# Twelve small stores of an attention and MoE kernel: from SyncE's queue to GpSimd's

## The chip, the cores and the metric

The kernel runs on one core of one Trainium2 chip. The metric is the device time of one execution in microseconds (us). A core has five instruction queues that run side by side and wait for each other by semaphores: TensorE (PE, with its weight loads PEld), VectorE (DVE), ScalarE (ACT), GpSimd (POOL) and SyncE (SP). SP does no arithmetic here; it issues DMA transfers. ACT and POOL can issue them too, from the same in-order queue in which their arithmetic stands.

## The reference, cut to what matters

```python
scores = scale * np.matmul(q, k.transpose(0, 1, 3, 2))      # 4 batches, 8 heads, 576 x 576, head size 64
cum = np.cumsum(np.maximum(s, 0.0), axis=-1)                # one running sum per head
bias = -(cum[:, :, :, None] - cum[:, :, None, :])
scores = np.where(causal, -1e9, scores + np.minimum(bias, 0.0))
attn = softmax(scores)                                      # with 1e-9 in the denominator
x = (attn @ v) put together as 2304 x 512
h = max(x @ w1, x @ w2, x @ w3) @ w_out                     # 512 -> 768 -> 512
y = ((h @ w_a) * (h @ w_b)) @ w2_out                        # 512 -> 1536 -> 512
```

All of it is float32. The running sums `cum` enter the scores as extra rows of the contraction: a row of sums on the side of k against a row of ones on the side of q, and the other way round.

## The kernel before, in words

**Stages.** Attention runs over four batches, each cut in two steps: R = 0 is the first 256 queries, R = 1 the other 320, and each step takes four pairs of heads. So there are eight steps. While a step's attention runs, TensorE is filled up with the first MoE layer's matmuls (line 826, tile `g`) of an earlier step. From about the middle of the run the second half follows: w_out, then the second MoE layer, with its products formed in a Strassen-like scheme.

**Plain and split scores.** In the first three steps (`NPLAIN = 3`) the scores are plain float32 matmuls, whose extra rows come from the DRAM tiles `ck` and `cq` (lines 500 to 520). From the fourth step on they are split: every operand is a rounded high part and a rest, and the sums are split as well. The high and low sums lie in DRAM tiles `kt` and `qt`, and rows of the tiles `KB2` and `QA2` are loaded from them by `k_tails` (line 572) and `q_tails` (line 577), on ACT's queue for the steps R = 1 and for the first pair of a step, on SP's else.

**The stores.** `store_tails` (line 209) makes the high part `hi` by an ACT cast (line 212) of the sums `cum`, leaves the rest in `cum` by a DVE subtraction (line 213), and calls `store_sums` (line 200) twice: six DMAs from `hi` and six from `cum`, to `kt` and `qt`. Each DMA reads 16 partitions. `store_sums` is called a third time earlier, in the lead-in (line 1207), for `ck` and `cq`. `hi` lies in the space that `KB2` takes later, `cum` in that of `KB1`; `preset` (line 224) fills `QA1`, `KB2` and `QA2` with constants by eight POOL memsets (lines 230 to 239).

**What else stands in the two queues.** SP issues nearly all loads: the weights of the first MoE layer, `wraw` (line 255, three staging buffers `wst`, each freed once the high and low part of a weight block have been made by lines 266, 269, 270, 81 and 92), and the q, k and v of coming pairs (line 509). POOL multiplies each block of exponentials by the reciprocal of its row sum (line 642, tiles `F` and `FJ`). The product is transposed by TensorE (lines 778, 780, 791) and goes from there into the product with v (line 760, `fpv`).

**The order.** The kernel lists its work as entries with a position in steps (`stream`), sorted, with priorities (`tc.high_priority`): attention of the first two steps 300, weights 200, MoE matmuls, `store_tails` and `preset` 0. A planner then fixes each queue's order at build time by its own estimate of durations; `issue_after` puts instructions behind a given one. On the chip each queue runs strictly in that order. `store_tails` has position 1.3 and `preset` 1.6; both are put behind the end of the last softmax listed before them:

```python
stream.append((1.3, 0, lambda: behind_sm(store_tails)))
stream.append((1.6, 0, lambda: behind_sm(preset)))
```

Of the kernel before, what the change touches and what calls it, by code (L numbers as in the profile page):

```python
# [29 lines left out]
def kernel(  # L30
# [18 lines left out]
    nc = tc.nc  # L49
# [18 lines left out]
    Q0 = 256  # L68
# [6 lines left out]
    def f(ap):  # L75
        return ap.bitcast(F32)
# [62 lines left out]
    kt = dram.tile([2, SR, 2, S], F32, name="kt")  # L139
    qt = dram.tile([2, SR, 2, N1], F32, name="qt")  # L140
# [26 lines left out]
    def early(nm, dt=F32):  # L167
        w = 2 * S if nm in ("KB1", "KB2") else QW
        return ap_.tile([P, w], dt, tag=nm, bufs=1, name=f"e{nm}")

    cum, sraw = early("KB1"), early("KB2")
# [25 lines left out]
            op0=ALU.mult, op1=ALU.add,  # L197
        )

    def store_sums(dk, dq, t):  # L200
        nc.sync.dma_start(dk[:, :, :Q0], t[64:80, : 2 * Q0].rearrange("r (h c) -> r h c", h=2))
        a, b = t[64:80, tl_], t[80:96, tl_]
        nc.sync.dma_start(dk[:, 0, Q0:], a)
        nc.sync.dma_start(dk[:, 1, Q0:], b)
        nc.sync.dma_start(dq[:, 0], a)
        nc.sync.dma_start(dq[:, 1, 0:64], b[:, 256:])
        nc.sync.dma_start(dq[:, 1, 64:], b[:, :256])

    def store_tails():
        hi = early("KB2", F32R)  # L210
        c = slice(0, 2 * Q0 + N1)
        nc.scalar.copy(hi[rr, c], cum[rr, c])
        nc.vector.tensor_tensor(cum[rr, c], cum[rr, c], f(hi[rr, c]), op=ALU.subtract)
        store_sums(kt[0], qt[0], f(hi))
        store_sums(kt[1], qt[1], cum)

    def heads(t, r0, r1, n):

# [797 lines left out]
    for stp in range(nsteps):  # L1016
        b, R = divmod(stp, 2)
# [18 lines left out]
    def behind_sm(fn):  # L1036
        with ExitStack() as es:
            for e_ in done_sm[-1]:
                es.enter_context(tc.issue_after(e_))
            fn()  # L1040

    stream.append((1.3, 0, lambda: behind_sm(store_tails)))
    stream.append((1.6, 0, lambda: behind_sm(preset)))

# [37 lines left out]
    def lead_in():  # L1082
# [119 lines left out]
        with tc.high_priority(4000):  # L1202
            fs(0)
            fs(1)
            with tc.issue_after(pend[-1][-1]):
                scan_tails()
            lead_rows.append(lambda: store_sums(ck, cq, cum))
            fetch(NP)
            fs(2)
            ts(0)  # L1210
            fs(3)
            sm_b(pend.pop(0))
            ts(1)
            pv(0)
            ts(2)
            pv(1)
            fetch(NP + 1)
            ts(3)
            wn()
            pv(2)  # L1220
            wn()
            sp(1)
            pv(3)
            wn(NL - 2)
# [731 lines left out]
```

## Time and profile before

| what | us |
|---|---|
| median of 3 runs | 881.88 |
| lowest, highest | 881.17, 883.26 |
| profiled execution, whole | 881.39 |
| profiled execution, span from first to last instruction | 879.3 |
| TensorE busy | 869.2 |
| VectorE busy | 631.2 |
| ScalarE busy | 401.7 |
| GpSimd busy | 198.1 |

The granted clock of TensorE is 1.00 of full speed over the span. Busy time counts what an engine computes; issuing a DMA and waiting on a semaphore are not counted. A row with a "q" behind the engine (SPq, ACTq) is the queue's own instruction, such as the issue of a DMA.

### The profile page before, as it was taken

What the parts mean: (1) busy time and instruction counts of PE and PEld (TensorE: products, weight loads), DVE (VectorE), ACT (ScalarE), POOL (GpSimd) and SP (SyncE); (2) the same over time, 40 slices, a digit from 0 to 9 for tenths busy, and PEclk for the clock granted to TensorE, in tenths of its full rate; (3) what the DMA queues carried; (4) which work ended last, traced back from release to release, by engine and by line L of the source; (5) the groups of instructions that cost most, each with busy time, mean ns of one, the idle gap of its engine ahead of it and who ended that gap; (6) DMA issues with size and microseconds to landing.
All of it is one profiled execution on the core that took longest, in us unless ns stands there. A gap on an engine that the chain in (4) does not pass through costs nothing.

```text
span 879.3 us, 16771 instructions
## 1 busy us (share of the span) xinstructions
PE 869.2 (99%) x6024; PEld 827.2 (94%) x6024; DVE 631.2 (72%) x1435; ACT 401.7 (46%) x872; POOL 198.1 (23%) x317
## 2 busy tenths in 40 slices
PE   8999999999999999999999999999999999999998
PEld 6667999899999998999999999999999999999998
DVE  7886555676767666665798867676766859987873
ACT  6686745575656545563554323232323224433321
POOL 6224312333423323200002111111111310322211
PEclk9999999999999999999999999999999999999999
DMA  7675634265224853474201134444442253353331
GB/s 226 197 204 174 179 121 127 74 189 152 64 86 137 245 171 117 135 289 154 108 12 61 46 111 150 151 150 151 150 150 102 103 188 121 110 164 127 97 120 49
DMA packets 68371, 120.07 MB, mean 137 GB/s; under 512 B 7024, under 2 KB 50784, under 8 KB 68288
## 3 DMA queue, kind: packets, MB, share of 16 engines
q1 hardware_dynamic: 61096, 111.60, 40.4%
q10 hardware_dynamic: 7192, 7.40, 2.5%
q8 instruction: 48, 0.79, 0.4%
q14 instruction: 35, 0.29, 0.1%
HBM read 87.95 MB, written 31.01 MB: 135 GB/s over the span
## 4 chain that ended last, share of the span: by engine, by line
PE 92%; DMA 2%; DVE 2%; ACT 1%; issue 1%; SPq 0%; POOL 0%; POOLq 0%; ACTq 0%; DVEq 0%
PE X L1322 29%; PE g L826 24%; PE Z L1322 15%; PE Y L1322 8%; PE fpv L760 5%; PE t L778 2%; DMA wraw<-in_moe_w_dram 2%; PE s L650 2%; PE s L651 2%; PE f L694 1%; PE ft L733 1%; PE W L1322 1%; PE sj L684 1%; PE tj L791 1%; PE sj L685 1%
## 5 line engine op out<-in xcount | busy, mean ns | idle before, releaser
L826 PE MATMUL g<-Xh,hg 128*128 128x256 f32 (+1 forms) x576 | 174.2, 306 | 1.9 <-POOL hg L88 0.8
L826 PE MATMUL g<-Xl,hg 128*128 128x256 f32 (+1 forms) x576 | 173.6, 302 | 0.0
L826 PE MATMUL g<-Xh,lg 128*128 128x256 f32 (+1 forms) x576 | 172.4, 301 | 0.0
L826 PEld LDWEIGHTS g<-Xh,hg 128*128 128x128 f32 x576 | 108.3, 189 | 5.9 <-ACT hg L81 1.5
L826 PEld LDWEIGHTS g<-Xh,lg 128*128 128x128 f32 x576 | 108.5, 189 | 3.0 <-issue 1.1
L826 PEld LDWEIGHTS g<-Xl,hg 128*128 128x128 f32 x576 | 108.8, 189 | 1.8 <-issue 0.7
L88 POOL TENSOR_SCALAR wh<-wval 128x256 fp32r<-128x256 f32 x77 | 39.9, 528 | 273.9 <-DVE wval L354 224.9
L1322 PE MATMUL X<-xh,wh 128*128 128x384 f32 x288 | 97.3, 338 | 0.0
L1322 PE MATMUL X<-xl,wh 128*128 128x384 f32 x288 | 96.9, 336 | 0.0
L1322 PE MATMUL X<-xh,wl 128*128 128x384 f32 x288 | 96.8, 337 | 0.0
L1322 PE MATMUL X<-woh,slot 128*128 128x256 f32 x408 | 76.6, 281 | 0.5 <-ACT ob L1369 0.5
L642 POOL TENSOR_SCALAR P<-P,rs 128x128 f32<-128x128 f32 (+2 forms) x80 | 50.4, 634 | 96.1 <-DVE rs L638 66.6
L367 DVE TENSOR_TENSOR slot<-hraw,slot 128x768 fp32r<-128x768 f32 x60 | 60.4, 1033 | 13.8 <-POOL slot L88 11.0
L367 DVE TENSOR_TENSOR u<-Z,u 128x384 f32<-128x384 f32 x72 | 39.6, 552 | 37.0 <-ACT u L1369 27.3
L1322 PEld LDWEIGHTS X<-woh,slot 128*128 128x128 f32 x408 | 64.3, 189 | 0.7 <-ACT ob L1369 0.7
L628 ACT ACTIVATE P<-P,nm 128x128 f32<-128x128 f32 (+2 forms) x80 | 46.6, 583 | 35.4 <-DVE nm L621 25.1
L835 DVE TENSOR_TENSOR hf<-g,hf 128x256 f32<-128x256 f32 (+1 forms) x96 | 43.6, 454 | 22.7 <-PE g L826 17.2
L1322 PE MATMUL X<-wol,slot 128*128 128x256 f32 x204 | 56.9, 280 | 0.0
L81 ACT ACTIVATE slot<-hraw 128x768 fp32r<-128x768 f32 x39 | 32.5, 845 | 51.4 <-DVE hraw L367 24.4
L1322 PEld LDWEIGHTS X<-xh,wh 128*128 128x128 f32 x288 | 54.0, 188 | 0.8 <-DVE u L367 0.3
L1322 PEld LDWEIGHTS X<-xl,wh 128*128 128x128 f32 x288 | 54.1, 188 | 0.0
L1322 PEld LDWEIGHTS X<-xh,wl 128*128 128x128 f32 x288 | 54.0, 188 | 0.0
(228 smaller groups left out, 2201.1 us busy)
## 6 DMA issues: line engine op xcount, KB each, us to landing
hT<-u SPq DMA_DIRECT2D x72, 192.0 KB
hraw<-hT SPq DMA_DIRECT2D x36, 384.0 KB
wraw<-in_moe_w_dram SPq DMA_DIRECT2D x18, 512.0 KB
wraw<-in_moe_w_out_dram SPq DMA_DIRECT2D x18, 512.0 KB
kraw<-in_kT_dram SPq DMA_DIRECT2D x24, 288.0 KB
wraw<-in_moe_w_a_dram SPq DMA_DIRECT2D x12, 512.0 KB
wraw<-in_moe_w_b_dram SPq DMA_DIRECT2D x12, 512.0 KB
st<-h1T SPq DMA_DIRECT2D x24, 192.0 KB
```

The source lines that it names most:

```text
L81: return nc.scalar.activation(o, i, AF.Copy, scale=scale)
L88: nc.gpsimd.tensor_scalar(o, i, scale, 1.0, op0=ALU.mult, op1=ALU.mult)
L367: return {"V": nc.vector, "P": nc.gpsimd}[e].tensor_tensor(o, a, b, op=op)
L628: e_ = nc.scalar.activation(pt[:, c0:c1], pt[:, c0:c1], AF.Exp, bias=first, scale=-1.0, accum_out=sm[:, g : g + 1],)
L642: n_ = nc.gpsimd.tensor_scalar(pt[:, c0:c1], pt[:, c0:c1], rs[:, g : g + 1], 1.0, op0=ALU.mult, op1=ALU.mult,)
L650: nc.tensor.matmul(ps, QA1[:, qs], KB1[:, h, ksl], start=True, stop=False)
L651: nc.tensor.matmul(ps, QA2[:, qs], KB2[:, h, ksl], start=False, stop=True)
L760: e_ = nc.tensor.matmul(ps[h * D : h * D + D, c0:n], w, x, start=(t == 0), stop=(t == len(mm[h]) - 1),)
L778: nc.tensor.transpose(ps[:, j * P : j * P + P], pt[:, j * P : j * P + P], ident)
L826: nc.tensor.matmul(ps[:, :n], w[:, kk, :], x[:, kk, :], start=(i == 0), stop=(i == len(mm) - 1),)
L835: st["V"] = nc.vector.tensor_tensor(hf, ps[:, :n], hf, op=ALU.max)
L1322: e_ = nc.tensor.matmul(ps[:, :n], w, x, start=(first and i == 0), stop=(i == len(mm) - 1), skip_group_check=not first,)
```

## The change

Both calls of `store_sums` in `store_tails` pass GpSimd's queue, so that their twelve DMAs are issued by POOL. The call of the lead-in (line 1207) keeps SP. What is stored, from where and to where is the same.

```diff
-    def store_sums(dk, dq, t):
-        nc.sync.dma_start(dk[:, :, :Q0], t[64:80, : 2 * Q0].rearrange("r (h c) -> r h c", h=2))
+    def store_sums(dk, dq, t, e=nc.sync):
+        e.dma_start(dk[:, :, :Q0], t[64:80, : 2 * Q0].rearrange("r (h c) -> r h c", h=2))
         a, b = t[64:80, tl_], t[80:96, tl_]
-        nc.sync.dma_start(dk[:, 0, Q0:], a)
-        nc.sync.dma_start(dk[:, 1, Q0:], b)
-        nc.sync.dma_start(dq[:, 0], a)
-        nc.sync.dma_start(dq[:, 1, 0:64], b[:, 256:])
-        nc.sync.dma_start(dq[:, 1, 64:], b[:, :256])
+        e.dma_start(dk[:, 0, Q0:], a)
+        e.dma_start(dk[:, 1, Q0:], b)
+        e.dma_start(dq[:, 0], a)
+        e.dma_start(dq[:, 1, 0:64], b[:, 256:])
+        e.dma_start(dq[:, 1, 64:], b[:, :256])
...
-        store_sums(kt[0], qt[0], f(hi))
-        store_sums(kt[1], qt[1], cum)
+        store_sums(kt[0], qt[0], f(hi), nc.gpsimd)
+        store_sums(kt[1], qt[1], cum, nc.gpsimd)
```

## Rows read from the trace of the kernel before

**Rows 1.** The page, part 1: busy us, share of the span, instructions of each engine.

```profile
PE 869.2 (99%) x6024; PEld 827.2 (94%) x6024; DVE 631.2 (72%) x1435; ACT 401.7 (46%) x872; POOL 198.1 (23%) x317
```

**Rows 2.** Windows: length, busy us (instructions) by engine, PEclk, DMA share, GB/s.

```profile
50.00:70.00 20.00, 18.90 (x127) 13.86 (x126) 17.61 (x49) 15.47 (x35) 5.52 (x7) 1.00 0.80 218
70.00:110.00 40.00, 40.00 (x285) 34.24 (x284) 23.09 (x96) 25.56 (x75) 16.72 (x33) 1.00 0.61 173
110.00:400.00 290.00, 289.74 (x2244) 272.46 (x2244) 190.76 (x566) 166.32 (x394) 78.16 (x130) 1.00 0.48 147
```

**Rows 3.** The chain that ended last, by time: start us, us, what.

```profile
49.09 5.71 DMA wraw<-in_moe_w_dram
...
57.47 5.32 DMA wraw<-in_moe_w_dram
```

**Rows 4.** Timeline of SP: start us, us, what; issues around the stores.

```profile
54.88 0.35 SPq L255 DMA_DIRECT2D wraw<-in_moe_w_dram  x1
55.27 0.60 SPq L201 DMA_DIRECT2D kt<-eKB  x1
...
57.47 0.35 SPq L255 DMA_DIRECT2D wraw<-in_moe_w_dram  x1
...
60.18 0.45 SPq L255 DMA_DIRECT2D wraw<-in_moe_w_dram  x1
...
65.69 0.42 SPq L207 DMA_DIRECT2D qt<-eKB  x1
```

**Rows 5.** SP's waits, 15 to 110 us: total us, times, longest us.

```profile
SPq L255 <- DVE lg L92: 11.6, 6, 6.3
...
SPq L207 <- DMA wraw<-in_moe_w_dram: 1.4, 1, 1.4
```

**Rows 6.** Timeline of POOL; in brackets the idle time before and what ended it.

```profile
50.66 0.69 POOL L642 TENSOR_SCALAR F<-F,rs 128x512 f32<-128x512 f32 x1 [0.48 <-PE g L826]
56.98 0.99 POOL L642 TENSOR_SCALAR F<-F,rs 128x512 f32<-128x512 f32 x1 [5.62 <-ACT hf L832]
58.44 0.58 POOL L642 TENSOR_SCALAR F<-F,rs 128x384 f32<-128x384 f32 x1 [0.48 <-DVE rs L638]
63.50 0.74 POOL L642 TENSOR_SCALAR FJ<-FJ,rs 128x576 f32<-128x576 f32 x1 [4.47 <-DVE rs L638]
66.66 1.38 POOL L642 TENSOR_SCALAR F<-F,rs 128x384 f32<-128x384 f32 x1 [2.42 <-DVE rs L638]
...
70.92 0.70 POOL L642 TENSOR_SCALAR F<-F,rs 128x512 f32<-128x512 f32 x1 [0.39 <-ACT hg L81]
...
71.64 1.06 POOL L232 MEMSET KB<- 64x1152 f32 x1
```

**Rows 7.** Timeline of PE: transposes of those blocks, and the idle place at 63.8.

```profile
59.09 0.60 PE L778 MATMUL t<-ident,F 128*128 128x128 f32 x4
...
63.83 1.12 PE L694 MATMUL f<-kraw,qvraw 66*128 66x512 f32 x2 [0.58 <-DVE nm L621]
...
69.17 0.49 PE L778 MATMUL t<-ident,F 128*128 128x128 f32 x3
```

**Rows 8.** Timelines of ACT and DVE: the two instructions that make the stored sums.

```profile
49.33 0.89 ACT L212 CAST eKB<-eKB 32x832 fp32r<-32x832 f32 x1
...
51.67 1.02 DVE L213 TENSOR_TENSOR eKB<-eKB,eKB 32x832 f32<-32x832 f32 x1
```

**Rows 9.** Timelines of ACT and PE: first load from `qt`, first split score.

```profile
75.16 0.50 ACTq L580 DMA_DIRECT2D QA<-qt  x1
...
109.11 0.29 PE L684 MATMUL sj<-KB,QA 128*128 128x288 f32 x1
```

**Rows 10.** Timeline of DVE: one operation, beside POOL's normalisation, alone, and beside its memset.

```profile
50.80 0.83 DVE L269 TENSOR_SCALAR wraw<-wraw 128x512 int32<-128x512 int32 x1 [0.34 <-DMA wraw<-in_moe_w_dram]
...
60.14 0.43 DVE L269 TENSOR_SCALAR wraw<-wraw 128x512 int32<-128x512 int32 x1
...
71.53 1.46 DVE L269 TENSOR_SCALAR wraw<-wraw 128x512 int32<-128x512 int32 x1 [0.81 <-DMA wraw<-in_moe_w_dram]
```

## The prediction

> **What bounds the kernel now.** I read the page's busy times first. TensorE is busy for 869.2 of a span of 879.3 us [rows 1], so all its idle time together is about 10 us, and a small change gains or loses only through that idle time. The table by windows says where it lies: from 50 to 70 us, the stretch in which the twelve stores are issued, PE is busy for 18.90 of 20 us, so 1.10 us are open; from 70 to 110 nothing is open, and from 110 to 400 only 0.26 us [rows 2]. The reader is to see there that VectorE, with 17.61 of 20 us, is nearly full in the stretch of the stores, that GpSimd, with 5.52, is mostly free, and that the DMA engines are busy for 0.80 of it.
>
> The chain of waits then tells what is late in this stretch: twice the landing of a weight block of the first MoE layer, of 5.71 and 5.32 us [rows 3]. The timeline of PE shows what is left of that: the longest gap between 50 and 70 us is 0.58 us, at 63.83 [rows 7]. From 70 us on PE is its own bound, so a delay before 70 us comes out at the end in nearly full size, and so would a gain.
>
> **What is removed from SP.** Twelve DMA issues, the first 0.60 us and the last 0.42 us long, stand in SP's queue between 55.27 and 66.11 us, with weight loads (line 255) in between [rows 4]. What matters is whether those loads would go out earlier. The load at 57.47 is the one on the chain. SP's waits for the weight loads are mostly for DVE's low parts (line 92), which free the staging buffers: 11.6 us over six waits [rows 5]. The last such operation before ends at 57.41 in DVE's timeline (56.72 + 0.69), and the store before the load had ended at 56.96, so 57.47 is set by the buffer: no gain. The load at 60.18 is the only one that can move: line 92 had freed a buffer at 59.57 (58.62 + 0.95), so it goes up to 0.61 us earlier. But DVE and ACT take up its block at 65.31 and 64.42, each directly behind other work, so nobody was waiting for it. The stores also take turns in completion counters with SP's other transfers, which is why one of them waits 1.4 us for the landing of an unrelated weight block [rows 5]; that wait holds up only stores, since the next weight load, at 64.81, is again released by DVE (63.69 + 1.10 = 64.79). Value taken: 0. Bounds: no loss, as nothing is added to SP; at most the 1.10 us that PE has open in the stretch as a gain.
>
> **What is added to POOL.** Twelve issues. The trace has no DMA issued by POOL, so the price of one is bounded from rows: from below by SP's shortest, 0.30 us (at 59.13 in its timeline), from above by POOL's memset of 64x1152, 1.06 us [rows 6], the dearest thing that POOL does there without reading. The nearest row in kind is SP's issue of the same transfer, 0.60 us, the nearest in engine is the memset; I take the dearer, since even this one fits: 12 x 1.06 = 12.7 us.
>
> The Trainium skill (DMA: Bandwidth & Descriptors, section Specifications) gives about 1 us to the first byte for GpSimd's path and about 0.6 for SyncE's, because GpSimd's cores compute the descriptors in software. No run here shows it yet; by that figure the twelve would be an estimated 12 us of POOL.
>
> Where do they go? `hi` is ready at 50.22 us and `cum` at 52.69 [rows 8]. POOL is idle for 5.62, 0.48, 4.47, 2.42 and 0.39 us ahead of the normalisations shown [rows 6], 13.4 us in all without the one left out at 69.05. So they fit into POOL's idle time before the memsets at 71.64, and a normalisation is late by at most the rest of one store, 1.06 us, if the planner lays them into the gaps. Each normalisation has slack before PE takes its block [rows 6, 7]: 59.09 - 57.97 = 1.12 us for the one at 56.98, 69.17 - 68.04 = 1.13 for the one at 66.66. So one store in the way is covered. If that cover is gone, every us more is a us of PE. Behind a POOL store are queued the normalisations and, after 71 us, the eight memsets of `preset`, and behind these the loads from `qt` at 75.16 on ACT's queue, where ACT's copies for PE stand too. Their data is needed only at 109.11 [rows 9], so a late landing of the stores has 34 us of cover; only a memset that is late by more than a us or two would hold up ACT. Value taken: 0.
>
> **What moves in the DMA engines.** The bytes are the same: per call six blocks of 16 rows with 512, 320, 320, 320, 64 and 256 columns of 4 bytes, 32 + 20 + 20 + 20 + 4 + 16 = 112 KB. On POOL the first six can start at 51.4 instead of 55.27, and then share the engines with the first late weight block rather than with the second [rows 3]. At the stretch's 218 GB/s [rows 2] that is 0.5 us off one and onto the other. Value taken: 0; bounds -0.5 to +0.5.
>
> **What DVE loses.** DVE and POOL hinder each other: line 269 takes 0.43 us alone and 1.46 us where it runs beside POOL's memset [rows 10], 1.03 us more. Five of these operations start between 51.4 and 71 us. If all met a store as they met the memset, DVE would lose 5.2 us, with 2.39 us idle in the stretch [rows 2], so 2.8 us would come out. If a store writes little, nothing is lost. The one at 50.80, beside the normalisation at 50.66, took 0.83 us, 0.40 more than alone [rows 6, 10]; I take one such loss that reaches PE: +0.4. Bounds 0 and +2.8.
>
> The Trainium skill (SBUF — State Buffer, section Who interferes with whom) says that GpSimd and a DVE operation in a two-port mode exclude each other for a whole instruction, and that descriptors made by GpSimd are held up by it. The 1.46 us agree with the exclusion; whether a store counts as the memset does, no run here shows.
>
> **Sum.** 0 + 0 + 0 + 0.4 on the profiled execution's own 881.39 us (span 879.3 and 2.1 around it): 881.8. This execution lies 0.49 us below the median of the runs shown, 881.88; set against the median the forecast is 882.3 us. Nothing in the 2.1 us around the span should change, though a queue that is used for the first time could add something there.
>
> **The rivals.**
>
> (a) *POOL's queue blocks (slower).* The planner, which doesn't know the chip's durations, may put a block of stores ahead of a normalisation that is already due. Place: the gap from 51.35 to 56.98. The gap and the slack of 1.12 hold 6.7 us, which is six stores at 1.06; from the seventh on PE is late. With all twelve in a row POOL is free at 51.35 + 12.7 = 64.1 and the block due at 56.98 comes 6.0 us too late; with nine, 2.8. For it: the stores have priority 0 but are ready from 50.2 on, while POOL's next work isn't. Against: the planner prefers attention, and on SP it spread the stores over 10 us. Taken in the middle +3: 885. Chance 0.20.
>
> (b) *DVE loses its full price (slower).* The bound above less what is already counted: +2.8, so 884.7. For it: DVE is 88% busy, and it makes the weight parts on which PE's gaps hang. Against: line 269 is five of about fifty operations there, and a store writes a few descriptors, not 64x1152 elements. This is the skill's rule taken at its word. It decides from about four collisions at 1.03 us. Chance 0.07.
>
> (c) *SP's relief counts (faster).* If the loads go out earlier after all, PE gets back its 1.10 us, and as much again in waits of PE's weight loads that the busy time hides; about -2.2: 879.7. For it: the chain goes through these loads. Against: the buffers set them. Chance 0.12.
>
> (d) *The move shows only in the order.* The planner reckons with other durations after 50 us and lays the queues of other engines out in another order, with a loss or gain of about 2 us that has nothing to do with the stores: 884 or 880. PE's open 0.26 us from 110 to 400 speaks against more. Chance 0.06, half on each side.
>
> **How the numbers follow.** Forecast 0.55, (a) 0.20, (b) 0.07, (c) 0.12, (d) 0.06. Within 0.2% is within 1.76 us of 881.88, about what a measurement of this kernel can tell from no change; the forecast lies in it whole (its own range is 881.2 to 883.6). So same 0.55; slower 0.20 + 0.07 + 0.03 = 0.30; faster 0.12 + 0.03 = 0.15. The range goes to 880.2 below, which leaves out most of (c), and to 885.5 above, which leaves out the larger half of (a): together about 0.2.
>
> **What would show it.** In the changed kernel's trace: twelve DMA issues on POOL, spread between 51 and 71 us, at 0.3 to 1.1 us each; normalisations of line 642 at most 1.1 us later than now, with PE's transposes waiting for none of them; the weight load at 60.18 about 0.6 us earlier, the one at 57.47 unmoved; line 269 longer than 0.43 us once or twice; PE's idle time from 50 to 70 us between 1 and 2 us. Wrong would be: PE waiting for line 642 by more than 1 us (a), DVE's idle time in the stretch gone (b), PE's idle time below 0.5 us and later stages starting earlier (c), or a difference that opens where no store is near (d).

## The result, and the profile after

Before 881.22 us (median of 7 runs, 880.34 to 883.26), after 886.22 us (7 runs, 884.20 to 886.96). The ratio is 1.0051, 95% interval 1.0039 to 1.0064: slower by about half a per cent, 4.5 us by the ratio and 5.0 us between the medians. The forecast was 882.3 us, its range ended at 885.5.

The page of the changed kernel first, part 1 and one queue of part 3, to be laid beside [rows 1]; then the windows that answer to [rows 2].

```profile
PE 874.0 (99%) x6024; PEld 831.7 (94%) x6024; DVE 630.3 (71%) x1435; ACT 401.9 (45%) x872; POOL 205.0 (23%) x329
...
q0 software_dynamic: 384, 0.23, 0.1%
```

```profile
50.00:70.00 20.00, 18.68 (x121) 14.59 (x118) 18.58 (x49) 14.13 (x30) 11.52 (x18) 0.93 0.75 226
70.00:110.00 40.00, 38.99 (x270) 31.00 (x270) 20.41 (x88) 24.80 (x70) 15.25 (x29) 0.99 0.45 137
110.00:400.00 290.00, 289.73 (x2245) 272.54 (x2244) 191.07 (x572) 166.22 (x397) 79.49 (x135) 1.00 0.49 150
```

POOL has twelve instructions more (329 against 317), and 384 packets of 0.23 MB have gone to a queue that the kernel before did not use. From 110 to 400 us PE is as full as before. From 70 to 110 PE was full, 40.00 of 40, and now has an idle us; its matmul records there fall from 285 to 270, which is a hint and no price, since other work stands in the window now.

The timeline of POOL (start us, us, what; in brackets the idle time before and what ended it) answers to [rows 6]:

```profile
52.99 0.69 POOL L642 TENSOR_SCALAR F<-F,rs 128x512 f32<-128x512 f32 x1 [0.49 <-PE g L826]
53.63 0.69 POOL L201 DMA_DIRECT2D kt<-eKB  x1
...
58.99 0.49 POOL L204 DMA_DIRECT2D kt<-eKB  x1 [1.28 <-DMA kt<-eKB]
...
61.22 0.48 POOL L206 DMA_DIRECT2D qt<-eKB  x1 [1.15 <-DMA kt<-eKB]
61.69 0.49 POOL L207 DMA_DIRECT2D qt<-eKB  x1
62.21 1.51 POOL L642 TENSOR_SCALAR F<-F,rs 128x512 f32<-128x512 f32 x2
```

All twelve stores stand in one row between the normalisation that came at 50.66 before and the one that came at 56.98 [rows 6]. A store costs POOL 0.48 to 0.69 us, about half of what the sum took. The ninth waits 1.28 us and the eleventh 1.15 us for the landing of an earlier one. These waits are the built program's: each store on POOL raises one of eight completion counters in turn, and from the ninth on a store waits for the counter that it shares with an earlier one. The block is 8.6 us long (53.63 to 62.18) where POOL had 5.62 us free.

The granted clock of this profile is not 1.00 throughout. It is 0.63 from 25 to 30 us and 0.69 from 30 to 35, so partly at the level of 1.2 GHz, before any store and behind five us in which PE was busy for 4.20 (before: 4.33, and the clock stayed); and 0.72 from 65 to 70, behind five us with 4.22. The first dip moves what follows by some 2.3 us (52.99 against 50.66 for the normalisation ahead of the stores). To see the change without it, the changed kernel was run once more. That profile (*again*) is at clock 1.00 from end to end, and the times of its stages can be set against those of before directly.

> The changed kernel once more, so that the others have it on the same chip. Theory 1 (the planner's order: it reckons the block of twelve POOL stores as long and lays the transposes behind it some 40 places later in PE's order), theory 2 (the block itself: the normalisations really come late and PE waits for them) and theory 3 (stores made by POOL cost by themselves: DVE loses the shared port, or the queue's first use costs) all expect 884 to 887 us. What it tells besides: whether the fall of TensorE's clock near 25 to 35 us, ahead of any store, comes back; I expect not, and the one at 65 to 75 us to come back.

Measured: 884.83 us (5 runs, 883.73 to 885.60), ratio 1.0036 (1.0023 to 1.0049), span 883.0 against 879.3. The loss is there at full clock. Its POOL timeline:

```profile
50.91 0.70 POOL L642 TENSOR_SCALAR F<-F,rs 128x512 f32<-128x512 f32 x1 [0.48 <-DVE rs L638]
51.55 0.69 POOL L201 DMA_DIRECT2D kt<-eKB  x1
...
56.66 0.49 POOL L204 DMA_DIRECT2D kt<-eKB  x1 [1.03 <-DMA kt<-eKB]
58.63 0.48 POOL L205 DMA_DIRECT2D qt<-eKB  x1 [1.49 <-DMA kt<-eKB]
...
60.10 1.25 POOL L642 TENSOR_SCALAR F<-F,rs 128x512 f32<-128x512 f32 x2
```

The normalisation due at 56.98 [rows 6] comes at 60.10. This profile is 0.25 us behind at the one ahead (50.91 against 50.66), so it is 2.9 us late: the block of the prediction's rival (a), in its place. But PE does not wait for it. The transposes of this block, at 59.09 before [rows 7], stand behind 26 matmuls of tile `g` in PE's new order and come at 68.03; from 55 to 75 us neither PE nor its weight loads wait for line 642 once:

```profile
62.49 1.12 PE L694 MATMUL f<-kraw,qvraw 66*128 66x512 f32 x2 [0.78 <-DVE nm L621]
...
68.03 0.60 PE L778 MATMUL t<-ident,F 128*128 128x128 f32 x4
```

So the lateness is only one of two things that the block did. The other is this planned order. The planner, too, reckons with a block on POOL, and it laid out PE anew: 872 of its 5728 rows differ from before (a moved row counts twice, where it was and where it is; the expectation of *split_a* counts 703 for the same kernel, so only the size of these counts tells), with the first 200 the same. ACT's and DVE's orders changed with it, by over a hundred rows each. How the MoE matmuls (tile `g`) are spread over the time shows it best. Windows with the instructions of tile `g` alone (length, then PE's busy us and count first), of the kernel before:

```profile
60.00:70.00 10.00, 3.25 (x18) 2.49 (x19) 0.42 (x1) 0.34 (x1) 1.00 0.64 201
...
90.00:100.00 10.00, 2.65 (x13) 1.88 (x12) 0.42 (x1) 0.43 (x1) 1.00 0.45 131
```

and of *again*:

```profile
60.00:70.00 10.00, 6.22 (x44) 5.21 (x42) 1.13 (x3) 0.35 (x1) 1.00 0.66 206
...
90.00:100.00 10.00, 0.28 (x1) 0.28 (x2) 0.00 (x0) 0.00 (x0) 1.00 0.28 80
```

`g` is what PE does while attention waits for a softmax. In the new order twice as much of it is used up at 60 to 70 us, and almost nothing is left at 90 to 100. What that does is plain in PE's timeline. Before:

```profile
89.31 0.82 PE L694 MATMUL f<-kraw 66*128 66x128 f32 x4
89.78 0.50 PE L826 MATMUL g<-Xl,hg 128*128 128x320 f32 x1
...
90.41 0.31 PE L826 MATMUL g<-Xh,lg 128*128 128x320 f32 x1
90.56 0.82 PE L694 MATMUL f<-kraw 66*128 66x128 f32 x4
91.22 0.93 PE L778 MATMUL t<-ident,F 128*128 128x128 f32 x7
91.98 1.48 PE L694 MATMUL f<-kraw 66*128 66x128 f32 x8
93.39 2.42 PE L760 MATMUL fpv<-PF,qvraw 128*64 128x320 f32 x20
```

*again*, the same stretch of attention:

```profile
90.33 0.90 PE L694 MATMUL f<-kraw 66*128 66x128 f32 x4
91.07 0.60 PE L778 MATMUL t<-ident,F 128*128 128x128 f32 x4
91.94 0.92 PE L694 MATMUL f<-kraw 66*128 66x128 f32 x4 [0.27 <-DVE nm L621]
92.90 0.66 PE L778 MATMUL t<-ident,F 128*128 128x128 f32 x4
94.20 0.55 PE L778 MATMUL t<-ident,F 128*128 128x128 f32 x3 [0.65 <-POOL F L642]
94.59 0.83 PE L694 MATMUL f<-kraw 66*128 66x128 f32 x4
95.48 2.42 PE L760 MATMUL fpv<-PF,qvraw 128*64 128x320 f32 x20
```

Scores (`f`) and transposes (`t`) follow each other with no `g` between them, and PE stands still for DVE's maximum (0.27 us) and for POOL's normalisation (0.65 us). From the second group of four scores to `fpv` it is 3.54 us here (91.94 to 95.48) and 2.83 us before (90.56 to 93.39), although one group of four fewer lies between here. At 60 to 70 us `g` itself comes too early: PE waits 0.37 and 0.58 us for DVE's low parts of the weights (line 92), and 0.78 us for a maximum.

So two theories stood after the first traces. **Lateness**: the block on POOL holds up a normalisation and PE waits for it, there or further on. **Order**: the planner's answer to the block, MoE matmuls used up too early, costs by itself, with the stores as its cause only in the plan. Beside them stood what else the change brings: SP's relief, and a DMA issued by POOL as such.

### The profile page after: what moved, and what is told of

The parts are those of the page before. It is cut to its first block, busy times and chain, and to the rows that moved or that the text cites. A ratio compares the mean times of both kernels' runs of the same rounds, so it can differ in the third digit from the quotient of the medians.

```text
span 885.2 us, 16787 instructions
## 1 busy us (share of the span) xinstructions
PE 874.0 (99%) x6024; PEld 831.7 (94%) x6024; DVE 630.3 (71%) x1435; ACT 401.9 (45%) x872; POOL 205.0 (23%) x329
## 4 chain that ended last, share of the span: by engine, by line
PE 92%; DVE 3%; DMA 2%; ACT 2%; issue 1%; POOL 0%; POOLq 0%; ACTq 0%; DVEq 0%
PE X L1322 29%; PE g L826 25%; PE Z L1322 15%; PE Y L1322 8%; PE fpv L760 5%; PE t L778 2%; PE s L650 2%; DMA wraw<-in_moe_w_dram 2%; PE s L651 2%; PE ft L733 1%; PE W L1322 1%; PE f L694 1%; PE sj L684 1%; DVE F L621 1%; PE sj L685 1%
## 5 line engine op out<-in xcount | busy, mean ns | idle before, releaser
L826 PE MATMUL g<-Xh,hg 128*128 128x256 f32 (+1 forms) x576 | 176.4, 310 | 1.8 <-POOL hg L88 0.8
L826 PE MATMUL g<-Xh,lg 128*128 128x256 f32 (+1 forms) x576 | 175.5, 307 | 0.4 <-DVE lg L92 0.4
L826 PEld LDWEIGHTS g<-Xh,hg 128*128 128x128 f32 x576 | 110.1, 192 | 6.3 <-ACT hg L81 1.7
L826 PEld LDWEIGHTS g<-Xh,lg 128*128 128x128 f32 x576 | 110.5, 193 | 2.5 <-DVE lg L92 0.9
L826 PEld LDWEIGHTS g<-Xl,hg 128*128 128x128 f32 x576 | 110.6, 192 | 1.6 <-issue 0.5
```

What stands on the lines that cost most here:

```text
L826: nc.tensor.matmul(ps[:, :n], w[:, kk, :], x[:, kk, :], start=(i == 0), stop=(i == len(mm) - 1),)
```

## The experiments

The ratio is always to the kernel before on the same chip, where it took 881.31 us (13 runs; *again*, *hi_only*, *late*, *after_pe*), 881.26 us (25 runs; *ext4*, *ext12*, *dummy480*, *split_a*) and 881.90 us (30 runs; the last four). The ratios are those of the record and not quotients of the medians; these lie elsewhere by up to 0.16 points (*ext12* 1.0037, *order_only* 1.0050).

**hi_only: six stores on POOL, six on SP.**

```diff
-        store_sums(kt[1], qt[1], cum, nc.gpsimd)
+        store_sums(kt[1], qt[1], cum)
```

> The six stores of the high sums on POOL, the six of the low sums on SP. The block is half as long (some 3 us at 0.49 each, which POOL's idle 5.6 us hold, and too few for a store to wait for another's landing), but PE's order is nearly that of the changed kernel: the transposes of the block at 57 us stand 14 places later than before (41 in the changed kernel). Theory 1: most of the loss stays, 884 to 886 us. Theory 2: 881 to 882 us. Theory 3: about half, 883.5 us.

Measured: 883.25 us (8 runs), 1.0028 (1.0015 to 1.0040). POOL's timeline, the last store and the next normalisation, and from DVE's timeline the reciprocal that this one needs:

```profile
57.26 0.48 POOL L207 DMA_DIRECT2D qt<-eKB  x1
59.87 0.93 POOL L642 TENSOR_SCALAR F<-F,rs 128x512 f32<-128x512 f32 x1 [2.12 <-ACT F L628]
```

```profile
59.50 0.15 DVE L638 RECIPROCAL rs<-rs 128x1 f32<-128x1 f32 x1
```

POOL is free 2.12 us before the normalisation starts, 0.2 us behind the end of the reciprocal; in the kernel before it is the same 0.2 us (reciprocal until 56.78, start at 56.98). The bracket names ACT, but these exponentials had ended at about 56.5. So the block holds up nothing here, and by the runs more than half of the loss remains. PE's order is that of the changed kernel but for 120 rows, and `g` has 5.98 us of PE at 60 to 70 and 0.16 at 90 to 100. That spoke for the order. The time alone did not decide, since it lies below what theory 1 expected and next to theory 3's 883.5; *ext4* and *split_d* below speak against theory 3.

**late: the same twelve stores listed behind a later softmax.**

```diff
     stream.append((1.3, 0, lambda: behind_sm(store_tails)))
+    stream.append((1.58, 0, lambda: behind_sm(store_later)))
```

`store_later` holds the two calls of `store_sums`.

> All twelve stores on POOL, but listed later, behind the softmax that stands just ahead of the memsets of preset, so that on POOL they follow the normalisations of that stretch in place of preceding them. PE's order is close to that of the kernel before. Theory 1: 880.5 to 882 us. Theory 2: the same, unless the memsets of preset come too late for ACT. Theory 3: the loss stays, 885 to 887 us.

Measured: 885.06 us (5 runs), 1.0044 (1.0029 to 1.0058). The block only moved. It stands from 73.19 to 80.97, with 1.79 us of waiting for a landing in it, ahead of the next normalisation due:

```profile
79.06 0.49 POOL L204 DMA_DIRECT2D kt<-eKB  x1 [1.79 <-DMA kt<-eKB]
...
82.07 0.58 POOL L648 TENSOR_SCALAR F<-F,rs 128x384 f32<-128x384 f32 x1
```

That one came at 75.44 before, and this profile is 1.64 us behind at the normalisation ahead of the block (72.56 against 70.92), so it is 5.0 us late. PE's order differs from before in some 128 rows only. Theory 1 expected no loss here, so this is a miss for it, and theory 3's 885 to 887 fits, though *split_d* below speaks against that theory. What is left is that lateness can cost, if there is enough of it. It is not priced by this run, since PE's weight loads wait 1.4 us for the landing of a q block in the same stretch. SP's new order by itself is not the reason: the planned order of SP in *split_d* (below) is the same, row for row, and *split_d* has neither this wait nor a loss.

**after_pe: two edges that should give the changed kernel the transposes' old place in PE's order.**

```diff
+                with tc.issue_after(hold[NP + 1, *{0: (3, 1), 2: (2, 1)}[i]]) if (b, R, m, g) == (0, 0, 4, 0) and i in (0, 2) else nullcontext():
```

> The changed kernel with two edges on PE: the first matmul of the gate (m = 4, g = 0) of the first step behind the transposes of the block at 57 us, its third behind those of the next block, as they stood in the kernel before. POOL's order is unchanged, the twelve stores still ahead of the two normalisations. Theory 1: PE waits some 2 to 3 us for the normalisation, but the attention behind it is early again: 882 to 884.5 us. Theory 2: nothing is won, 886 us or more, since PE now waits for the late block at once. Theory 3: 886 us.

Measured: 889.39 us (4 runs), 1.0091 (1.0067 to 1.0115). The edges did not give the old order back (922 rows differ from it); the planner put scores early instead, and PE is busy for only 5.36 of 10 us at 60 to 70; its weight loads wait 2.7 us for DVE's maximum there. The time fits theory 2's "886 us or more", but with this other order it decides nothing between the theories, and shows only that a worse order can cost still more.

**ext12 and ext4: all stores on SP, and twelve or four other DMAs on POOL**, each from 16 partitions of a constant to scratch memory.

```diff
         store_sums(kt[1], qt[1], cum)
+        for j in range(12):
+            nc.gpsimd.dma_start(junk[j], ident[64:80, 0:128])
```

> The same with twelve extra DMAs on POOL, all stores still on SP. PE's planned order is exactly that of the changed kernel. Theory B: the whole loss, 884 to 886.5 us, though nothing was taken from SP. Theory S (the loss comes from SP, whose weight loads go out in another order and at other times once the stores are gone): 881 to 882 us. Theory D: 884 to 886 us as well.

> The kernel before, all its stores on SP, plus four extra DMAs on POOL ahead of the normalisation at 57 us: 16 rows of 128 columns of the identity to a scratch tensor, which nothing reads. The planned order of all engines is that of before but for a handful of places. Theory B (a block of POOL work ahead of the normalisations is what costs, by the planner's order and by real lateness): four issues take some 2.2 us and fit into the idle 5.6 us: 881 to 882 us. Theory D (a DMA issued by POOL costs by itself, through DVE's port or the queue): a third of the loss or, for a first-use cost, all of it: 882.5 to 885 us.

Measured: *ext12* 884.54 us (4 runs), 1.0053 (1.0038 to 1.0068); *ext4* 881.38 us (10 runs), 1.0002 (0.9987 to 1.0017). *ext12* keeps SP as it was and moves no sums, and it costs what the change costs. So neither SP's relief nor what is stored is needed for it. Its PE order is the changed kernel's, row for row, and the block looks the same:

```profile
50.84 4.02 POOL L218 DMA_DIRECT2D junk<-ident  x8
56.88 1.50 POOL L218 DMA_DIRECT2D junk<-ident  x3 [2.02 <-DMA junk<-ident]
...
59.18 1.25 POOL L645 TENSOR_SCALAR F<-F,rs 128x512 f32<-128x512 f32 x2
```

*ext4* leaves PE's order almost alone (6 rows) and no loss shows, though POOL issues DMAs there too. A first use of that queue shows no price.

**dummy480: stores on SP, and twelve memsets of 64x480 on POOL**, which write rows that are not stored.

```diff
+        for _ in range(12):
+            nc.gpsimd.memset(f(hi[0:64, :480]), 0.0)
```

> The kernel before, all its stores on SP, plus twelve memsets of 64 x 480 on POOL in the place of the moved stores, about half a us each like a store; they write partitions that nothing reads. The planned order of PE, DVE, ACT and SP is exactly that of before; on POOL eight stand ahead of the normalisation at 57 us, one and three behind it. Theory B: if they start at 51.4 us the eight take 4 us of the idle 5.6 and nothing is late, 881 to 882 us; if the first has to wait for something else, the normalisations are late by as much and PE with them, 883 to 886 us, with PE's order unchanged. Theory D: 881 to 882 us, there is no DMA in it.

Measured: 881.54 us (10 runs), 1.0006 (0.9993 to 1.0019). Eight of them fill 4.70 us of the gap; the orders of PE, DVE, ACT and SP are those of before, row for row. That POOL is busy there shows no price.

These left order and lateness tangled in the changed kernel itself. The next three kernels take them apart: no DMA on POOL, stores on SP, memsets in place of the stores, with and without the new order, with and without a late normalisation. Their edits:

```diff
# order_only: seven memsets of 64x720
+        for _ in range(7):
+            nc.gpsimd.memset(f(hi[0:64, :720]), 0.0)
# late_only: five memsets of 64x800 behind a read of a weight block that lands late
+            tap_i[:] = [nc.gpsimd.tensor_scalar(tap[0:64], f(raw[0:64, 0:1, 1]), 1.0, 1.0, op0=ALU.mult, op1=ALU.mult).ins]
+        with tc.issue_after(tap_i[0]):
+            for _ in range(5):
+                nc.gpsimd.memset(f(hi[0:64, :800]), 0.0)
# order_and_late: the same with six of 64x720
```

> The twelve stores stay on SyncE as before; POOL gets seven memsets of 64x720 in the stores' place, which store nothing and write only rows that are not stored. The planner reckons them as a block and lays PE's order out nearly as it does with the twelve POOL stores (114 of 5728 PE rows differ from that order, 870 differ from the order before). On the chip six of them should take about 4.5 us (eight of 64x480 took 4.70), so they fit into POOL's gap of 5.62 us and the normalisation is not late. Theory 'order': the new planned order costs by itself, 882.8 to 884, PE less busy in 60 to 70 and 90 to 100 us. Theory 'lateness' (only the late normalisation costs): 881 to 882. Theory 'DMA' (only DMAs issued by POOL cost): 881 to 882.

> The stores stay on SyncE; PE's, DVE's, ACT's and SP's planned orders are row for row those of the kernel before. POOL reads one element of a weight block that lands at about 54.8 us and then does five memsets of 64x800 (about 0.8 us each by the rows of 64x480 and 64x1152) ahead of the normalisation that stood at 56.98, which should so come at about 59.0, 2 us late, of which 1.1 us were slack. Theory 'lateness': about 0.9 us or more is lost, 882 to 884. Theory 'order': 881 to 882.

> The planned orders of PE, DVE, ACT and SP are those of order_only (2 of 5728 PE rows differ); on POOL the read of the weight block that lands at about 54.8 us stands ahead of five memsets of 64x720, so that the normalisation comes about 1.7 us late, as in late_only. No DMA on POOL, stores on SyncE. If both theories hold and add up: order_only's loss plus late_only's, about 884 to 885.5, near the changed kernel's. If only lateness counts: as late_only. If only the order counts: as order_only.

Measured:

| kernel | PE rows that differ from before | normalisation late | us (runs) | ratio (95%) |
|---|---|---|---|---|
| *late_only* | 0 | 1.7 us | 881.36 (12) | 0.9996 (0.9983 to 1.0009) |
| *order_only* | 870 | no | 886.30 (6) | 1.0036 (1.0020 to 1.0053) |
| *order_and_late* | 872 | about 1.3 us | 884.54 (12) | 1.0030 (1.0015 to 1.0045) |

The new order without a late normalisation costs 0.36%, as *again* did; its 886.30 us lie above the 884 that theory 'order' expected, and of the two stretches expected only 90 to 100 us loses, while PE is full at 60 to 70. With the order kept, 1.7 us of lateness show no loss (-1.5 to +0.8 us by the interval). The order and the lateness together come out no slower than the order alone, though the intervals would leave room for some 2 us more. (The 1.3 us of *order_and_late*: the normalisation starts at 60.50, in *order_only* at 60.48, whose profile is 1.28 us further behind at the one ahead.)

The granted clock does not explain this. Dips ahead of the block stand in the profiles of kernels without a loss too (*ext4*, *late_only*, *split_d*), and half of the 30 runs of the kernel before have a mean clock under 0.998. Among runs with a mean clock of 0.998 or more the medians are 881.56 us before (15 runs), 880.88 *late_only* (11), 883.93 *order_and_late* (8) and 886.56 *order_only* (3). Counted from the normalisation ahead of the block to the end of the span, which leaves these dips out, the profiles have 828.6 us before, 828.3 in *dummy480*, 828.0 in *late_only*, 827.4 in *split_d*, 826.7 in *split_a*, and 832.1 in *again*, 832.2 in *ext12*, 831.2 in *order_only*, 830.2 in *late*, but only 829.5 in *hi_only*; it is one profile each, and those without a loss differ by 1.9 us.

POOL in *late_only*; lines 644 to 649 of these kernels are line 642, moved by the added lines:

```profile
51.73 0.69 POOL L648 TENSOR_SCALAR F<-F,rs 128x512 f32<-128x512 f32 x1 [0.48 <-PE g L832]
55.26 0.27 POOL L326 TENSOR_SCALAR tap<-wraw 64x1 f32<-64x1 f32 x1 [2.83 <-DMA wraw<-in_moe_w_dram]
55.47 4.32 POOL L219 MEMSET eKB<- 64x800 f32 x5
59.78 1.91 POOL L648 TENSOR_SCALAR F<-F,rs 128x512 f32<-128x512 f32 x2
```

This profile is 1.07 us behind at the first of these (51.73 - 50.66), so the normalisation is 59.78 - 56.98 - 1.07 = 1.7 us late. PE does wait for it, and yet no loss shows in the time:

```profile
61.01 0.66 PE L784 MATMUL t<-ident,F 128*128 128x128 f32 x4 [1.09 <-POOL F L648]
...
63.68 1.02 PE L700 MATMUL f<-kraw,qvraw 66*128 66x512 f32 x2
```

The idle 0.58 us before the scores at 63.83 [rows 7] are gone: PE waited 1.09 us earlier, and the maximum that it had waited for is there in time. In *order_only* POOL is free 1.09 us before the normalisation starts, again 0.2 us behind the end of DVE's reciprocal:

```profile
54.59 4.80 POOL L217 MEMSET eKB<- 64x720 f32 x6
60.48 0.96 POOL L644 TENSOR_SCALAR F<-F,rs 128x512 f32<-128x512 f32 x1 [1.09 <-ACT F L630]
```

```profile
60.13 0.15 DVE L640 RECIPROCAL rs<-rs 128x1 f32<-128x1 f32 x1
```

and yet PE's windows lose at 90 to 100 us, *order_only* first, *late_only* second:

```profile
90.00:100.00 10.00, 9.08 (x56) 6.15 (x57) 4.41 (x28) 6.75 (x21) 3.41 (x7) 1.00 0.22 72
```

```profile
90.00:100.00 10.00, 10.00 (x75) 8.21 (x74) 4.79 (x34) 7.77 (x28) 3.93 (x9) 1.00 0.36 105
```

**split_a and split_d: the twelve stores on POOL in groups of 4, 3, 2, 3 or of 3, 3, 3, 3**, each group listed behind another softmax.

```diff
+        store_next(3)
...
+    stream.append((1.4, 0, lambda: behind_sm(lambda: store_next(3))))
+    stream.append((1.5, 0, lambda: behind_sm(lambda: store_next(3))))
+    stream.append((1.58, 0, lambda: behind_sm(lambda: store_next(3))))
```

> The twelve stores on POOL as in the change, but listed in four groups of 4 (one of them already behind the first normalisation), 3, 2 and 3, each behind another softmax, so that each group stands in another of POOL's gaps. PE's order differs from before in 65 lines, from 703 in the changed kernel. Theory B: no normalisation is late by more than about a us: 881 to 882.5 us. Theories S and D: the loss stays, 884 to 886 us.

> The twelve stores on POOL in four groups of three, of which the later three are listed behind later softmaxes, so that no more than three stand ahead of a normalisation and none is the ninth within a few us. PE's order differs from before in 60 of 5728 rows. If the block and what it does to order and lateness are the whole cause, this costs nothing: 880.5 to 882.5. If a DMA on POOL costs something by itself: 884 to 886, as with twelve in a row.

Measured: *split_a* 882.44 us (10 runs), 1.0015 (0.9996 to 1.0034); *split_d* 881.17 us (12 runs), 0.9994 (0.9983 to 1.0005). In *split_d* the stores fit into the gaps, as the prediction had it:

```profile
54.90 1.66 POOL L207 DMA_DIRECT2D kt<-eKB  x3
60.10 0.93 POOL L649 TENSOR_SCALAR F<-F,rs 128x512 f32<-128x512 f32 x1 [3.55 <-DVE rs L645]
...
62.41 1.49 POOL L207 DMA_DIRECT2D qt<-eKB  x3
```

PE's order is that of before but for 60 rows, `g` has 3.55 us at 90 to 100, and no loss shows from the move of the stores. No gain shows either. The Trainium skill (DMA: Bandwidth & Descriptors, section Rules for kernel authors) says that spreading DMAs over the issuing engines brings no bandwidth and only saves issue time; here, with SP rid of all twelve, not even that shows in the time. No version beat the kernel before.

The `g` windows at 90 to 100 us sort all these kernels by the result: those without a loss that shows have 2.7 to 4.2 us of `g` there (before, *dummy480*, *ext4*, *late_only*, *split_a*, *split_d*), the others 0 to 1.8. At 60 to 70 us the changed kernel, *again*, *hi_only*, *ext12*, *order_only* and *order_and_late* have 5.9 to 7.2 us of `g` and those without a loss 2.8 to 4.9; but *late* (4.7) and *after_pe* (3.5) lose without much `g` there. That the place of `g` is what costs is read from the timelines; no run moved `g` alone.

## Why the prediction was wrong

**The step that failed** is the one under POOL: "they fit into POOL's idle time before the memsets at 71.64, and a normalisation is late by at most the rest of one store, 1.06 us, if the planner lays them into the gaps", value taken 0. The planner laid all twelve in one row. The sum had counted gaps as if instructions flowed into them; on an in-order queue they stand where the plan put them. And the sum holds the order of all other queues fixed: it has no term for what the planner does with PE's work when POOL's load changes. The runs put the cost in that missing term: 3.2 us (*order_only*: 0.36% of 881.9; interval 1.8 to 4.7) with no normalisation late. In *split_d*, where the stores were put into the gaps by hand, the 0 is right.

**Rival (a), "POOL's queue blocks"**, named the block, its place and a lateness (6.0 us beyond the slack; 2.9 measured, 1.8 beyond it) and lay nearest in time (885), at 0.20. That nearness is luck. Its own sign, "PE waiting for line 642 by more than 1 us", is absent in the changed kernel from 55 to 75 us; it is there in *late_only* (1.09 us), where (a) would have taken 1.7 - 1.12 = 0.6 us. No loss shows there, though the interval doesn't exclude 0.6.

**Rival (d), "the move shows only in the order"**, is the mechanism that the runs show: the queues of other engines were laid out anew, for 2 us by the prediction and 3.2 us measured. It had 0.06, half of that for a loss, on the argument that PE has only 0.26 us open from 110 to 400 us [rows 2]. The time is lost ahead of that, and there the prediction reads PE's 40.00 of 40 us [rows 2] as "from 70 to 110 nothing is open". That bounds a gain, not a loss: a full PE was the merit of one particular order, with `g` matmuls between the scores.

**The price of a store** was taken as 1.06 us by the memset; it is 0.48 to 0.69, nearer to SP's 0.60 [rows 4]. That was too dear, but the wait that was left out made up for part of it: twelve issues sum to 6.1 us in *again*, and 1.03 + 1.49 us of waiting for landings come on top.

**DVE** lost nothing to the stores (rival b), and the 0.4 us that the sum took for it did not appear. Line 269 in the changed kernel, beside the block of stores:

```profile
56.71 0.43 DVE L269 TENSOR_SCALAR wraw<-wraw 128x512 int32<-128x512 int32 x1
```

The 0.43 us are those of the operation alone [rows 10]; in *again* two more beside stores took 0.42 and 0.43 (at 54.59 and 59.53). The Trainium skill (SBUF — State Buffer, section Who interferes with whom) says that GpSimd and a DVE operation in a two-port mode exclude each other; no trace here shows that for a store of this size.

**SP's relief** (rival c) earned nothing: no gain shows in *split_d*, which has it, and *ext12* lacks it and loses about the same. **Around the span** nothing was added either: 884.83 - 883.0 = 1.8 us in *again* against 2.1 before.

**What stays open**: whether lateness adds anything in the changed kernel further on, where PE waits 0.65 us for a normalisation at 94.20 in *again*. Its ratio, 1.0051, lies above *order_only*'s 1.0036 and *again*'s 1.0036, but all intervals overlap; *late* says that about 5 us of lateness, at another place, may cost. *order_only* is also not the changed kernel's order to the row (114 rows differ, the transposes at 68.03 among them); only *ext12* has that, with its own late normalisation. Which of the three new orders costs, PE's, ACT's or DVE's, was not taken apart. Why the planner answered the block in just this way was not looked into, and two figures show how little tells: five memsets of 64x800 behind the read leave every other queue as it was, six of 64x720 lay out 872 rows of PE's order anew.

## What to carry to other kernels

Where a planner fixes the order, ask of a moved instruction first what it does to the plan: compare the planned order of the busiest engine before and after, because that, not the instruction, can be most of the cost. A stretch in which the bounding engine is full is not safe; look at what fills it, and whether that filler is used up elsewhere. To move small work to another in-order queue, hand it over in pieces no longer than the gaps: the same twelve stores cost 0.36 to 0.51% in one row, and in threes no loss shows.

## What the runs showed of the hardware

A store of 16 partitions, issued by POOL, holds POOL's queue for 0.48 to 0.69 us and lands some 5 us after its issue (median 4.8 to 5.2 us by size in the changed kernel and *again*; 3.1 to 4.6 in *late*). Eight in a row take about 4 us, and the ninth, which the program makes wait for the counter of the first, stands for 1.28 us in the changed kernel, 1.03 in *again*, 1.79 in *late*, 2.02 in *ext12* with other data. In groups of three no store waited. SP's issues of the same stores had been 0.30 to 0.61 us.

When one normalisation was delayed by 1.7 us, PE stood still 1.09 us for it and 0.58 us less at the next wait on the chain; in the time no loss shows.
